# Moving small matmul groups in a fused FFT and gated feed-forward kernel: opening steps and batch 1's slots

## The chip, the cores and the metric

The kernel runs on one core of a Trainium2 chip. The metric is the device time of one execution in microseconds. Five engines work side by side and synchronise by semaphores: TensorE (PE; its weight loads are PEld), VectorE (DVE), ScalarE (ACT), GpSimd (POOL) and SyncE (SP), which issues transfers. A ratio in this document is the mean time of one kernel's fast runs over that of the other's in the same rounds, so it isn't quite the ratio of the medians quoted.

## The reference, cut to what matters

```python
X = np.fft.fft(np.fft.fft(x, axis=1), axis=2).real          # x: 8 x 3008 x 256
x = X.reshape(8 * 3008, 256)
gate = np.maximum(x @ w_gate, 0.0)                           # 256 x 1536
return (gate * (x @ w_val)) @ w_out                          # 1536 x 256
```

## The kernel before

The FFT over the sequence is done in two stages of matmuls (stage one over 94 rows, a shuffle, stage two over 32). The FFT over the 256 columns never happens by itself: it is multiplied into the weights, which is the "W fold". Real input makes half of the rows mirror images of the other half, so one gate tile G and one value tile V serve both: first the direct product is taken, then one more matmul with the mirrored weights `wm` is added to the same tile and the mirrored product is taken. In names, `cs` is 0 or 1 and picks one of two halves of a transform (for the weights, wc or ws). An *evacuation* is the copy of a finished matmul result out of its accumulator buffer. TensorE *stands* when it waits with nothing to do.

A *step* (or slot) is one of 8 x 3 x 12 tiles of 512 columns (batch, block, 128 hidden features). The twelve opening steps (batch 0, block 0) have no output matmuls yet, and the W folds for the features 512 to 1535 are done beside them. Everything else that must happen in between is hung on a slot number (`nyquist`, not shown, is a group of twelve one-column matmuls; `load_x` issues half of a batch's input, a plain part in the queue it is given and a gather of the mirrored part in GpSimd's):

```python
def fold_w(n, i, cs, ps=None):                 # W fold: two f32 matmuls, 64 weight columns each
    ps = ps or spare("psw")                    # one of two spare buffers, in turn
    ...
    nc.scalar.copy((wc, ws)[cs][i][:, sl_], ps[:])
    if cs and (n or i):
        scale_w(n, i, ps)                      # VectorE: wm, from the same buffer

def upright(blk, cs, evac):  ...               # 4 matmuls of 128 columns, then a copy to t4
def rotate(b, a0=0, a1=NKA, evac=...):  ...    # the "turn": one tiny matmul, then a copy
def stage2(b, blk, cs, evac):                  # 4 matmuls of 128 columns, then a copy to pq
    ...
    if cs == 1 and (b or blk):
        row = view(Nd, ...)                    # one 1 KB row goes to DRAM ...
        nc.sync.dma_start(out=row, in_=pq[0:1, 1, :])
        nc.sync.dma_start(out=nbt[b, blk][:], in_=view(row, 0, [[0, 128], [1, 512]]))  # ... and comes back on 128 partitions

for t in range(NF + 1):                        # the opening steps; NF = 12
    if t:      mirror_gate(t - 1)
    if t < NF: gate(t)
    if t:
        value(t - 1, 2)                        # adds the mirrored weights to V of step t-1
        mirror_h(t - 1, 1, nc.vector, pair(t - 1, "V"))
    if t < NF:
        value(t, 0); value(t, 1)
        direct_h(t, 1)                         # VectorE; must read V before value(t, 2) adds to it
        between(t)                             # what is hung on slot t
```

`nb` (the row on 128 partitions) is read by the product E of later steps: `E = nb * af + V`. GpSimd folds the next batch's input (`fold`, 23 pieces a batch) while it also makes one mirrored product per two steps; `FIRST` is how many pieces of batch 1 come before the steps, and `pace` deals out the others.

## Time and profile before

| | before |
|---|---|
| median of the first 4 runs | 625.49 us (625.27 to 626.45) |
| span of the profiled run | 623.2 us |
| first W fold inside the steps | 22.25 us from the start |
| from there to the mirrored V matmul of step 11 | 27.04 us |
| from there to the last matmul | 567.98 us |

The last three rows cut the span at matmuls: the start-up, the opening steps, all else. (Some 6 us from the last matmul's start to the end of the span are left out.) The lines of the profile itself are in the prediction below. In these lines `x4` is a count, the bracket at the end is the engine's idle time just before the line and what ended it, and `xcount` entries are merged neighbours.

### The profile page before, as it was taken

The page shows a single profiled execution, that of the slowest core. Times are in us where ns is not written, and L with a number is a line of the kernel's source. Part 1 is how long each engine was busy: PE and PEld are TensorE (multiplying, and loading weights), DVE is VectorE, ACT ScalarE, POOL GpSimd, SP SyncE. Part 2 cuts the span into 40 slices and gives each one's busy share as a digit, 9 for nine tenths or more (in the row PEclk, how much of TensorE's full clock was granted, in tenths as well). Part 3 has the DMA queues.
Part 4 walks back from the last instruction along what each step waited for, and adds up shares of the span by engine and source line. Part 5 has one row for each costly group of instructions (what it writes and reads, how often), then busy time and mean ns, then how long its engine had stood idle before and what let it go on. Part 6 is the DMA issues. An engine that isn't in the chain of part 4 may idle for free.

```text
span 623.2 us, 11964 instructions
## 1 busy us (share of the span) xinstructions
PE 614.0 (99%) x4284; PEld 409.6 (66%) x4284; DVE 538.2 (86%) x654; ACT 444.6 (71%) x855; POOL 519.9 (83%) x447
## 2 busy tenths in 40 slices
PE   8999999999999999999999999999999999999996
PEld 5336666766666666666667666666666666666665
DVE  8677997899889898888988998898988889899991
ACT  8667777777777767767677767767677776766661
POOL 8987998998989898998989989898988865565665
PEclk9999999999999999999999999999999999999998
DMA  7885274525553183613825255531832134212114
GB/s 169 240 161 118 61 191 113 137 66 160 118 139 84 34 235 83 151 36 89 212 75 126 64 158 123 135 90 34 226 89 49 34 85 117 60 34 67 34 35 100
DMA packets 42038, 67.44 MB, mean 108 GB/s; under 512 B 5877, under 2 KB 31774, under 8 KB 39962
## 3 DMA queue, kind: packets, MB, share of 16 engines
q1 hardware_dynamic: 37162, 50.61, 32.3%
q0 software_dynamic: 4656, 15.88, 10.7%
q8 instruction: 33, 0.54, 0.4%
q14 instruction: 27, 0.22, 0.1%
q10 hardware_dynamic: 160, 0.20, 0.1%
HBM read 38.85 MB, written 30.17 MB: 111 GB/s over the span
## 4 chain that ended last, share of the span: by engine, by line
PE 96%; DVE 2%; ACT 1%; issue 0%; POOL 0%; POOLq 0%; DVEq 0%
PE po L683 40%; PE V L634 20%; PE G L619 10%; PE G L620 10%; PE G L626 10%; PE psw L333 2%; PE ps L162 2%; PE ps L271 2%; DVE h L647 0%; PE pst L240 0%; PE ps L216 0%; ACT t L230 0%; ACT back L197 0%; PE ps L166 0%; DVE wm L327 0%
## 5 line engine op out<-in xcount | busy, mean ns | idle before, releaser
L654 POOL TENSOR_TENSOR h<-gm,E 128x992 bf16<-128x992 f32 (+1 forms) x138 | 320.1, 2319 | 81.8 <-DVE E L661 50.4
L683 PE MATMUL po<-wo,h 128*128 128x256 bf16 (+2 forms) x2304 | 328.5, 272 | 0.0
L683 PEld LDWEIGHTS <-h 128*128 128x128 bf16 (+2 forms) x2304 | 231.4, 103 | 105.9
L628 ACT ACTIVATE gm<-G 128x496 f32<-128x496 f32 (+1 forms) x288 | 170.6, 592 | 94.6 <-PE G L626 87.8
L647 DVE TENSOR_TENSOR h<-gs,V 128x1024 bf16<-128x1024 f32 (+3 forms) x150 | 173.8, 1159 | 58.7 <-PE V L634 39.7
L641 DVE SCALAR_TENSOR_TENSOR E<-nb,af,V 128x496 f32<-128x496 bf16 (+1 forms) x276 | 190.2, 731 | 2.2 <-PE G L620 2.2
L621 ACT ACTIVATE gs<-G 128x497 f32<-128x497 f32 (+2 forms) x288 | 169.6, 589 | 24.7 <-PE G L620 24.7
L661 DVE SCALAR_TENSOR_TENSOR E<-E,V 128x992 f32<-128x992 f32 (+1 forms) x138 | 164.5, 1192 | 0.0
L619 PE MATMUL G<-pq,wc 128*128 128x497 bf16 (+2 forms) x288 | 107.9, 375 | 0.0
L620 PE MATMUL G<-pq,ws 128*128 128x497 bf16 (+2 forms) x288 | 107.9, 375 | 0.0
L626 PE MATMUL G<-pq,wm 128*128 128x496 bf16 (+1 forms) x288 | 107.9, 375 | 0.0
L634 PE MATMUL V<-pq,ws 128*128 128x497 bf16 (+2 forms) x288 | 85.4, 375 | 0.9 <-DVE E L641 0.9
L634 PE MATMUL V<-pq,wc 128*128 128x497 bf16 (+2 forms) x288 | 85.4, 375 | 0.0
L620 PEld LDWEIGHTS <-ws 128*128 128x128 bf16 x288 | 28.2, 98 | 32.7
L696 ACT COPY os<-po 128x512 f32<-128x512 f32 x63 | 37.0, 587 | 14.6 <-PE po L683 12.6
L634 PEld LDWEIGHTS <-wc 128*128 128x128 bf16 x288 | 28.2, 98 | 20.0 <-issue 1.6
L114 POOL TENSOR_TENSOR eo<-xla 94x256 bf16<-94x256 f32 x56 | 40.4, 733 | 0.7
L619 PEld LDWEIGHTS <-wc 128*128 128x128 bf16 x288 | 28.2, 98 | 18.1 <-DVE pq L278 0.8
L114 POOL TENSOR_TENSOR eo<-xlb 94x256 bf16<-94x256 f32 (+1 forms) x42 | 34.5, 822 | 0.9
L111 POOL TENSOR_TENSOR xla<-xla,xha 94x510 f32<-94x510 f32 x28 | 32.9, 1175 | 2.2
L177 ACT CAST t<-ps 96x512 bf16<-96x512 f32 x56 | 32.7, 584 | 2.4 <-PE ps L162 0.2
L626 PEld LDWEIGHTS <-wm 128*128 128x128 bf16 x288 | 28.1, 98 | 4.1 <-issue 1.6
(142 smaller groups left out, 370.8 us busy)
## 6 DMA issues: line engine op xcount, KB each, us to landing
out_dram<-os SPq DMA_DIRECT2D x124, 128.0 KB
Td<-t SPq DMA_DIRECT2D x7, 768.0 KB
t<-Td SPq DMA_DIRECT2D x7, 768.0 KB
out_dram<-os SPq DMA_DIRECT2D x82, 64.0 KB
xla<-in_x_dram SPq DMA_DIRECT2D x7, 720.0 KB
xlb<-in_x_dram SPq DMA_DIRECT2D x6, 640.0 KB
nb<-Nd SPq DMA_DIRECT2D x23, 128.0 KB
out_dram<-os SPq DMA_DIRECT2D x40, 48.0 KB
```

Of the source, the lines that this page charges most:

```text
L114: yield eng.tensor_tensor(e1[:, :, k:k + H], x1[:, :, 0:H], free(x1, D, [DX, n], [-1, H]), op=op)
L619: nc.tensor.matmul(G[:, ds], lhsT=wc[0][:, fs], rhs=pq[:, 0, ds], start=True, stop=False)
L620: nc.tensor.matmul(G[:, ds], lhsT=ws[0][:, fs], rhs=pq[:, 1, ds], start=False, stop=True)
L621: nc.scalar.activation(pair(t, "gs")[:, t % 2, ds], G[:, ds], ACTF.Relu)
L626: nc.tensor.matmul(G[:, cols], lhsT=wm[0][:, f * 128:(f + 1) * 128], rhs=pqt[b, blk][:, 1, cols], start=False, stop=True, skip_group_check ...
L628: nc.scalar.activation(pair(t, "gm")[:, t % 2, cols], G[:, cols], ACTF.Relu)
L634: nc.tensor.matmul(pair(t, "V")[:, t % 2, cs], lhsT=w[:, f * 128:(f + 1) * 128], rhs=pqt[b, blk][:, min(k, 1), cs], start=(k == 0), stop=( ...
L641: nc.vector.scalar_tensor_tensor(pair(t, "E")[:, t % 2, cols], nbt[b, blk][:, cols], af[:, f:f + 1], pair(t, "V")[:, t % 2, cols], op0=ALU ...
L647: nc.vector.tensor_tensor(pair(t, "h")[:, k, 0, 0:ds.stop - ds.start], pair(t, "gs")[:, k, ds], pair(t, "V")[:, k, ds], op=ALU.mult)
L654: eng.tensor_tensor(free(pair(t, "h")[:], 1024 * (t % 2) + 512 + w - 1, [1024, n], [-1, w]), pair(t, "gm")[:, k, cols], val[:, k, cols], o ...
L661: nc.vector.scalar_tensor_tensor(E[:, :, cols], E[:, :, cols], 2.0, V[:, :, cols], op0=ALU.mult, op1=ALU.subtract)
L683: nc.tensor.matmul(po[0:m, i, :], lhsT=pair(t - f + ff, "h")[:, ff % 2, sg, g * 128:g * 128 + m], rhs=wo[:, ff, :], start=(ff == 0), stop= ...
```

## The change

Its intent: turns and second-stage matmuls of batch 0 stand beside the W folds, two evacuations leave VectorE, batch 1's half with the row comes first, its input is loaded ahead of the first fold piece, and its slots move up.

```diff
-FIRST = 15
+FIRST = 17
...
+        load_x(1, 1, pl)
         first = fold(1, pl)
         next(first)
-        load_x(1, 1, pl)
...
     for n in (1, 2):
-        for k, t in enumerate(((0, 1, 2, 3), (4, 5, 6, 7))[n - 1]):
-            at(t, fold_w, n, k // 2, k % 2)
-    for t, blk, cs, e in ((2, 1, 1, "dve"), (4, 1, 0, "dve"), (6, 2, 1, "dve"), (8, 2, 0, "dve")):
-        at(t, upright, blk, cs, e)
-    at(3, rotate, 0, 4, 8)
-    at(7, rotate, 0, 8, NKA)
-    for t, blk, cs, e in ((5, 1, 1, "act"), (9, 2, 1, "act"), (10, 1, 0, "dve"), (11, 2, 0, "act")):
-        at(t, stage2, 0, blk, cs, e)
+        t = 4 * n
+        at(t - 4, fold_w, n, 0, 0)
+        at(t - 3, fold_w, n, 0, 1)
+        at(t - 3 if n == 1 else t - 4, upright, n, 1, "act" if n == 1 else "dve")
+        at(t - 2, rotate, 0, 4 * n, 4 * n + 4)
+        at(t - 2, fold_w, n, 1, 0)
+        at(t - 2, upright, n, 0, "dve")
+        at(t - 1, fold_w, n, 1, 1)
+        at(t - 1, stage2, 0, n, 1, "act")
+        at(t + 1 if n == 1 else t, stage2, 0, n, 0, "act")
     at(8, nyquist)
-    plan = {0: (12, 13, 14, 16, 19, 22, 23, 24), 1: (4, 5, 7, 10, 14, 18, 20, 21)}
+    plan = {0: (12, 13, 14, 15, 17, 20, 21, 22), 1: (4, 5, 7, 10, 14, 18, 20, 21)}
...
-        sh, tr, t2 = (22, 28, (29, 30, 32, 34, 35, 37)) if b else (25, 30, (31, 32, 33, 34, 35, 37))
+        sh, tr, t2 = (22, 28, (29, 30, 32, 34, 35, 37)) if b else (23, 29, (30, 31, 32, 34, 35, 37))
...
-            at(t0 + k, stage2, b + 1, i // 2, i % 2, "act")
+            at(t0 + k, stage2, b + 1, i // 2, 1 - i % 2, "act")
-            for half, k in enumerate((5, 24) if b else (14, 31)):
+            for half, k in enumerate((5, 24) if b else (14, 26)):
...
-        paced["due"] += 0 if t < 12 else 0.8 if t < 23 else 0.75 if t < 54 else 23 / 36
+        paced["due"] += 0 if t < 12 else 0.75 if t < 22 else 0.68 if t < 54 else 23 / 36
```

## The prediction

> **What bounds the kernel now.** I read part 1 of the page first, then the waits, then TensorE's timeline from start to start.
>
> ```profile
> PE 614.0 (99%) x4284; PEld 409.6 (66%) x4284; DVE 538.2 (86%) x654; ACT 444.6 (71%) x855; POOL 519.9 (83%) x447
> ```
>
> TensorE has no neighbour: in a span of 623.2 us only 9.2 us are not covered by its matmuls. That number is not yet a ceiling, because a matmul's box is longer than the place it takes: one of 496 columns is 0.37 us long but its successor starts 0.21 us later. So I took every start-to-start distance and subtracted the columns at 2.4 GHz. From 60 us on the remainder is 0.33 to 0.43 us per 20 us, which is streaming at full speed, except for one 20 us stretch with 1.40 us, where one distance is 1.02 us too long. Before that the remainder is 2.8 us (20 to 40 us) and 2.6 us (40 to 60 us). Only these two places can give anything; the change touches both. First place, TensorE's timeline of the twelve opening steps (batch 0, columns: start, length, engine, line, operation):
>
> ```profile
> 24.62 1.08 PE L333 MATMUL psw<-wst,cd 128*64 128x512 f32 x4
> 25.63 0.38 PE L626 MATMUL G<-pq,wm 128*128 128x496 bf16 x1
> ...
> 26.27 0.37 PE L634 MATMUL V<-pq,wm 128*128 128x496 bf16 x1
> ...
> 26.99 1.08 PE L333 MATMUL psw<-wst,cd 128*64 128x512 f32 x4
> ...
> 32.23 1.08 PE L333 MATMUL psw<-wst,cd 128*64 128x512 f32 x4 [0.17 <-DVE wm L327]
> ...
> 45.73 0.37 PE L634 MATMUL V<-pq,wm 128*128 128x496 bf16 x1
> ...
> 47.51 0.37 PE L634 MATMUL V<-pq,wm 128*128 128x496 bf16 x1
> ...
> 48.13 0.39 PE L271 MATMUL ps<-m,t 128*128 128x128 bf16 x4
> ...
> 49.29 0.37 PE L634 MATMUL V<-pq,wm 128*128 128x496 bf16 x1 [0.53 <-DVE h L647]
> ```
>
> A step with a W fold lasts 26.99 - 24.62 = 2.37 us when nothing else stands in it: the fold 1.01, six matmuls of 0.21, and some 0.1 of unhidden weight load. TensorE is the limit there. A step without a fold (9 to 11) lasts 49.29 - 47.51 = 1.78 us, as did the one before (47.51 - 45.73), although its matmuls need only 1.25 us plus 0.25 for a second-stage group. What sets 1.78 is in VectorE's timeline:
>
> ```profile
> 46.20 0.67 DVE L654 TENSOR_TENSOR h<-gm,V 128x496 bf16<-128x496 f32 x1 [0.53 <-PE V L634]
> 46.79 0.67 DVE L647 TENSOR_TENSOR h<-gs,V 128x496 bf16<-128x496 f32 x1
> 47.37 0.68 DVE L278 CAST pq<-ps 128x512 bf16<-128x512 f32 x1
> 47.98 0.67 DVE L654 TENSOR_TENSOR h<-gm,V 128x496 bf16<-128x496 f32 x1
> ```
>
> The mirrored matmul into V starts at 45.73; VectorE's mirrored product follows 0.47 later; the direct product of the next tile comes 0.59 after it; the next mirrored matmul waits for that one and starts 0.72 later: 0.47 + 0.59 + 0.72 = 1.78. This is a loop between two engines. The evacuation in the third line stands inside its slack and costs nothing: the last loop has no evacuation on VectorE and has the same length.
>
> Second place, the first step of batch 1. SyncE's queue, then VectorE, then TensorE:
>
> ```profile
> 89.30 0.97 SPq L93 DMA_DIRECT2D xlb<-in_x_dram  x2
> 92.76 0.24 SPq L282 DMA_DIRECT2D Nd<-pq  x1
> 98.68 0.35 SPq L283 DMA_DIRECT2D nb<-Nd  x1
> ```
>
> ```profile
> 98.68 1.20 DVE L647 TENSOR_TENSOR h<-gs,V 128x994 bf16<-128x994 f32 x1 [0.37 <-PE V L634]
> 101.65 1.37 DVE L641 SCALAR_TENSOR_TENSOR E<-nb,af,V 128x496 f32<-128x496 bf16 x2 [1.77 <-PE G L620]
> ```
>
> ```profile
> 103.07 0.58 PE L634 MATMUL V<-pq,ws 128*128 128x496 bf16 x2 [0.85 <-DVE E L641]
> ```
>
> The row of second-stage results (cs=1 half) goes to DRAM and comes back as the broadcast nb. It is issued behind 752 KB of x; its write takes 98.68 - 92.76 = 5.9 us until nb can be issued, and nb arrives about 101.6. The wait of 1.77 is put down to a matmul that had long been done (101.18), so it is the DMA. TensorE loses 1.02 us by the start-to-start count (0.85 in the view). Nothing after it loses any.
>
> **What the Trainium skill says.** "Perfetto Trace Analysis", Identifying the Most-Contended Engine: matmul busy share is not a good measure, since matmuls are pipelined; the trace agrees (0.37 against 0.21), hence the counting of starts. "TensorE: Matmul & The Clock Gate", Back-to-back issue gap: N/2.4 + 2.5 ns, 209 ns for 496 columns; the trace has 0.21. "PSUM — Partial Sum Buffer", PSUM bank collisions raise a hardware error: no two engines in one bank and quadrant at once. So ScalarE's copy of a fold and VectorE's scaled copy of it run one after the other: copy 25.75 to 26.34, scale 26.36 to 27.11, and the buffer is free 2.5 us after the fold began. "DMA: Bandwidth & Descriptors", Issuing engines are not separate DMA queues: all transfers share 16 engines and interleave; a 1 KB row needing 5.9 us behind x agrees.
>
> **The change part by part.** No instruction is added or removed; two evacuations move from VectorE to ScalarE.
>
> *Opening steps.* Steps 1 to 8 held four upright groups, two turns, the nyquist group and one second-stage group; steps 9, 10, 11 held one second-stage group each. Now all four second-stage groups are in steps 3, 5, 7, 8. So three groups (0.24, 0.25, 0.25 with the one-column matmuls and a trifle of issue: 0.74 us) leave steps where the 1.78 loop hid them, and enter steps where TensorE is the limit. Against that, waits go: 0.24 before the fold at 32.23 and 0.25 before the upright group at 42.61 (each for the scaled copy of the fold two buffers earlier), 0.05 at 37.46; in sum 0.54. New ones come, because the two spare buffers still alternate and a fold's buffer is free only 2.55 us (for a bf16 group) to 2.62 us (for a fold) after the fold began. Placing the new order by hand from 23.26: the turn of step 2 comes 0.05 too early, the fold of step 6, whose predecessor in the same buffer began 2.4 us before, waits 0.22, the others under 0.03. Sum to step 9: + 0.74 - 0.54 + 0.27, some + 0.5; following it step by step with rounding gives step 9 at 43.9 instead of 43.3. Then three loops of 1.78 in either kernel. So batch 0's opening becomes **0.55 us longer**, not shorter.
>
> *Row and x of batch 1.* The cs=1 half of block 0 moves from slot 32 to slot 30: 91.72 to about 87.7, plus 0.55 = 88.2. Its copy ends near 89.4, the row goes out near 89.9 behind the stores of 86.95. Even with 5.9 us for the write and 2.6 for the broadcast nb lands at 98.4; VectorE can use it from 99.9 + 0.55. The x half that stood in front of the row is issued at slot 26, some 9 us earlier. So the 1.02 us go whole: **-1.0 us**.
>
> *Slots moved up, x before the fold, FIRST and pace.* GpSimd loses 1.48 us waiting for x at 30.9; the issue of the other half (2.8 us) now fills this, which pays for the two extra fold pieces (about 2.1 us). The last pieces of batch 1's fold should end near 66.7 (71.3 now), and stage one asks for them near 68 to 72.5. The shuffle starts at about 74 instead of 77.84; its two transfers took 4.8 and 4.3 us, so it is back by 83 and the turn at slot 29 (about 85.9) finds it; now 87.0 meets 87.63. At the slower pace later folds end up to 0.8 piece (about 2 us) later; the least slack I find for the sixth product of batch 2 is 5.3 us (132.2 against 137.5). Worth on the path: **0**.
>
> Sum: + 0.55 - 1.02 = -0.47 us of 625.5, 625.0 us.
>
> **Rivals.** (1) *The opening gains.* If evacuations on VectorE lengthened steps 9 to 11, removing them would give those steps' waits back (0.27 + 0.28 + 0.70 by the start-to-start count): 623.2 to 623.8 in all. For it: the view blames VectorE's product. Against it: two loops, one with and one without an evacuation, are both 1.78. (2) *ScalarE becomes the bound of steps 1, 3, 5, 7*, with two copies beside two activations: four operations at a spacing of 0.48 are 1.9 us, below 2.6, but they delay the mirrored product by 0.5 us of a slack of about 0.8. If it binds, + 0.2 to + 0.5 per step: 626 to 627. (3) *A new wait in batch 1*: fold pieces or the shuffled tile late for the earlier slots, since x, stores and shuffle now overlap: up to + 1, cancelling the second gain: 626.0.
>
> **Range and chances.** The two sums are both fractions of a microsecond; the three runs of before spread over 1.2 us. I place the range a little lopsided to the fast side for rival 1: 624.0 to 626.1. A change of 2% would be 12.5 us, more than all the idle time TensorE has; slower by that needs a mechanism that I don't see. Faster 0.005, same 0.985, slower 0.01.
>
> **What would show it.** After: steps without fold still 1.78 apart from one mirrored V matmul to the next; the first V matmul of slot 12 at about 49.8 (49.29 now); a wait of some 0.2 before the fold of step 6; no gap of TensorE between 100 and 105, with E in VectorE's timeline following its predecessor directly and the row's write issued near 90. It is wrong if steps 9 to 11 fall below 1.7, if the opening ends before 49.3, if TensorE still waits for E at batch 1, or if a new wait appears between 60 and 100.

## The result

The changed kernel took 625.16 us (median of 4 runs, 624.65 to 625.70) against 625.49 us; ratio 0.9992, interval 0.9975 to 1.0009. Repeated later in 5 rounds: 625.02 against 625.54 us, ratio 0.9992, interval 0.9978 to 1.0005. By its times it is the same (the interval reaches from 1.6 us faster to 0.6 us slower); by the traces the whole stretch from the first W fold in the steps to the last matmul went from 595.02 to 594.65 us, which is 0.37 us less, and again 594.66 in the second trace of the changed kernel. The profiled run of the first result happens to have the later start-up (23.05 us), so its span, 623.9 us, is longer than that of before.

Part 1 of the changed kernel's page:

```profile
PE 612.0 (98%) x4252; PEld 409.3 (66%) x4284; DVE 536.7 (86%) x652; ACT 445.5 (71%) x857; POOL 520.0 (83%) x447
```

TensorE's count is 4252 and not 4284: 32 matmul records are missing from this trace, while the weight loads are all there. That makes holes of 0.22 us, exactly one matmul long, at regular places in a start-to-start count, and 2 us less of busy time. Neither is real. VectorE has two instructions fewer and ScalarE two more: the two evacuations.

TensorE's timeline of the opening steps, after (columns as in the prediction):

```profile
25.42 1.08 PE L333 MATMUL psw<-wst,cd 128*64 128x512 f32 x4
26.44 0.40 PE L240 MATMUL pst<-perm,t 128*128 128x128 bf16 x4
...
38.78 1.08 PE L333 MATMUL psw<-wst,cd 128*64 128x512 f32 x4 [0.20 <-DVE wm L327]
...
47.18 0.37 PE L634 MATMUL V<-pq,wm 128*128 128x496 bf16 x1 [0.24 <-DVE h L647]
...
48.96 0.37 PE L634 MATMUL V<-pq,wm 128*128 128x496 bf16 x1 [0.36 <-DVE h L647]
...
50.74 0.37 PE L634 MATMUL V<-pq,wm 128*128 128x496 bf16 x1 [0.79 <-DVE h L647]
```

In the second line an upright group follows the fold, where in the kernel before the next G matmul followed (25.63): TensorE fills such a step, so the group adds its own time. The third line has the new wait of step 6. The last three are 1.78 us apart as before, and the idle time before them has grown (0.24 and 0.36 where the view of before showed none, 0.79 where it showed 0.53): the groups that had stood there were free. VectorE, after:

```profile
47.66 0.67 DVE L654 TENSOR_TENSOR h<-gm,V 128x496 bf16<-128x496 f32 x1 [0.53 <-ACT gs L621]
48.24 0.66 DVE L647 TENSOR_TENSOR h<-gs,V 128x496 bf16<-128x496 f32 x1
49.44 0.67 DVE L654 TENSOR_TENSOR h<-gm,V 128x496 bf16<-128x496 f32 x1 [0.53 <-PE V L634]
```

The evacuation that stood between the second and third line is gone, and the third line still starts 1.78 after the first. SyncE's queue and VectorE at batch 1, after:

```profile
83.02 1.70 SPq L93 DMA_DIRECT2D xlb<-in_x_dram  x2
...
90.73 0.23 SPq L282 DMA_DIRECT2D Nd<-pq  x1
93.46 0.34 SPq L283 DMA_DIRECT2D nb<-Nd  x1
```

```profile
100.14 1.20 DVE L647 TENSOR_TENSOR h<-gs,V 128x994 bf16<-128x994 f32 x1 [0.41 <-PE V L634]
101.24 1.37 DVE L641 SCALAR_TENSOR_TENSOR E<-nb,af,V 128x496 f32<-128x496 bf16 x2
```

The row leaves at 90.73 (92.76 before, although this run started 0.8 us later), its write takes 93.46 - 90.73 = 2.7 us and not 5.9, and E follows its predecessor without a wait. TensorE has no standing there.

### The profile page after: what moved, and what is told of

It reads as the page before. It is cut to its first block, busy times and chain, and to the rows that moved or that the text cites. A ratio compares the mean times of both kernels' runs of the same rounds, so it can differ in the third digit from the quotient of the medians.

```text
span 623.9 us, 11929 instructions
## 1 busy us (share of the span) xinstructions
PE 612.0 (98%) x4252; PEld 409.3 (66%) x4284; DVE 536.7 (86%) x652; ACT 445.5 (71%) x857; POOL 520.0 (83%) x447
## 4 chain that ended last, share of the span: by engine, by line
PE 96%; DMA 1%; POOL 1%; issue 1%; DVE 1%; ACT 0%; POOLq 0%; DVEq 0%
PE po L683 40%; PE V L634 19%; PE G L619 10%; PE G L626 10%; PE G L620 10%; PE psw L333 2%; PE ps L162 2%; PE ps L271 2%; DMA lo<-in_x_dram 1%; POOL hi L132 0%; DVE h L647 0%; PE pst L240 0%; PE ps L216 0%; PE ps L166 0%; POOL lo L129 0%
## 5 line engine op out<-in xcount | busy, mean ns | idle before, releaser
L619 PE MATMUL G<-pq,wc 128*128 128x496 bf16 (+2 forms) x287 | 107.6, 375 | 1.2
L634 PE MATMUL V<-pq,ws 128*128 128x496 bf16 (+2 forms) x280 | 83.7, 374 | 0.0
L634 PE MATMUL V<-pq,wc 128*128 128x496 bf16 (+2 forms) x266 | 80.7, 374 | 0.0
```

The costliest lines, as they stand in the source:

```text
L619: nc.tensor.matmul(G[:, ds], lhsT=wc[0][:, fs], rhs=pq[:, 0, ds], start=True, stop=False)
L634: nc.tensor.matmul(pair(t, "V")[:, t % 2, cs], lhsT=w[:, f * 128:(f + 1) * 128], rhs=pqt[b, blk][:, min(k, 1), cs], start=(k == 0), stop=( ...
```

## The experiments

All twelve traces, cut at the same three matmuls (us). Single runs: their times are not compared closely, only their traces.

| kernel | start-up | opening | rest | opening + rest |
|---|---|---|---|---|
| before | 22.25 | 27.04 | 567.98 | 595.02 |
| after | 23.05 | 27.69 | 566.96 | 594.65 |
| opening_only | 22.38 | 27.69 | 568.39 | 596.09 |
| batch1_only | 22.53 | 27.04 | 566.96 | 594.00 |
| evac_only | 22.20 | 27.04 | 567.72 | 594.76 |
| loop_filled | 22.58 | 26.19 | 567.21 | 593.40 |
| x_slot_only | 22.97 | 27.03 | 572.23 | 599.26 |
| cs_first_only | 23.24 | 27.18 | 567.63 | 594.81 |
| slots_only | 22.49 | 27.69 | 566.96 | 594.66 |
| x_behind | 22.67 | 27.69 | 566.96 | 594.65 |
| after_again | 22.37 | 27.70 | 566.96 | 594.66 |
| loop_filled_again | 22.71 | 26.19 | 567.21 | 593.40 |

The theory is that of the prediction: the opening loses, batch 1's row gains, the other slots are worth nothing on the path. Its rivals are the three of the prediction.

### opening_only: the opening's order alone

Edit: on the kernel before, only the two blocks of `at(...)` lines of the opening steps from the diff above.

> Before, with the change's order of the twelve opening steps alone. My theory: three second-stage groups leave the loop of 1.78 us and enter steps that TensorE fills, so from the first W fold in the steps to the last mirrored V matmul of step 11 it takes 27.6 to 27.7 us (27.04 before), TensorE still stands about 1.0 us for E at batch 1, and the whole is 0.6 us slower than before (626.1). Rival 1 (the opening gains because evacuations leave VectorE): under 26.5 us there and 624.3 in all.

Measured: 625.95 us against 625.35 (4 and 9 runs), ratio 1.0008, interval 0.9993 to 1.0023. By the times that is the same within noise. By the trace the opening takes 27.69 us, 0.65 more than before, and TensorE stands 1.14 us for E at batch 1 (and 0.27 us at the turn of slot 30, see cs_first_only below). Rival 1 would have had under 26.5 us, and falls.

### batch1_only: all but the opening's order

Edit: on the changed kernel, the opening's `at(...)` lines of before.

> The changed kernel with the old order of the opening steps. My theory: the opening is back at 27.0 us, no standing of TensorE near 100 to 105 us, so 1.0 us faster than before and 0.6 faster than the changed kernel: ratio 0.9983 to before. Rival 1: as slow as before less 1.0, but slower than the changed kernel. Rival 3 (a new wait in batch 1): any gap of TensorE over 0.3 us between 50 and 105 us other than missing matmul records.

Measured: 624.33 us against 625.35 (5 and 9 runs), ratio 0.9986, interval 0.9972 to 1.0000. The opening is back at 27.04 us exactly, the rest at 566.96 exactly. The two parts of the change add up: + 0.65 in the opening, - 1.02 in the rest. Between 50 and 105 us no gap of TensorE over 0.3 us is left, so rival 3 does not occur here.

### evac_only: two evacuations moved and nothing else

```diff
-    for t, blk, cs, e in (..., (8, 2, 0, "dve")):      # upright
+    for t, blk, cs, e in (..., (8, 2, 0, "act")):
-    ..., (10, 1, 0, "dve"), ...                        # stage2
+    ..., (10, 1, 0, "act"), ...
```

> Before, with only the two evacuations (second upright group of block 2, cs=0 half of block 1) given to ScalarE in their old slots. My theory: the mirrored V matmuls of steps 8 to 11 stay 1.78 us apart and the opening stays at 27.0 us. Rival 1: the spacing of steps 9 and 10 falls below 1.6 us, the opening to under 26.5 us.

Only one of these two is an evacuation that the change moves: the cs=0 half of block 1. The change's other one is the first upright group of block 1, in step 1; here the one of step 8 is moved instead, just before the steps that rival 1 speaks of.

Measured (one run, 624.71 us): the spacings of the last three mirrored V matmuls are 1.79, 1.78 and 1.78 us, and the opening is 27.04 us. Taking work off VectorE in these steps changes nothing. What rival 1 would call VectorE's load is a loop between VectorE and TensorE. In this run the standing at batch 1 was 0.48 us and not 1.02: the arrival of nb varies from run to run (1.14 in opening_only). Another 0.27 us stands at the turn of slot 30, as in opening_only.

### loop_filled: the groups where the loop leaves room

```diff
-    (the change's opening block)
+        for k in range(4):
+            at(4 * n - 4 + k, fold_w, n, k // 2, k % 2)
+    at(1, upright, 1, 1, "act")
+    at(3, upright, 1, 0, "act")
+    at(8, upright, 2, 1, "act")
+    at(8, rotate, 0, 4, 8)
+    at(9, stage2, 0, 1, 1, "act")
+    at(9, upright, 2, 0, "dve")
+    at(10, stage2, 0, 1, 0, "act")
+    at(10, rotate, 0, 8, NKA)
+    at(11, nyquist)
+    at(11, stage2, 0, 2, 1, "act")
+    at(18, stage2, 0, 2, 0, "act")
```

(The last one uses the buffer that the output matmuls are not using, as later batches do.)

> The changed kernel, with the opening groups put where the 1.78 loop leaves TensorE 0.5 us a step: nothing but the two upright groups of block 1 beside W folds; turns, block 2's upright groups, second stage and nyquist in steps 8 to 11, the cs=0 half of block 2 in slot 18. My theory: the opening takes 25.8 us (27.04 before, 27.69 after), slot 18 costs 0.25, batch 1 keeps its gain: 2.0 us faster than before, ratio 0.9968, 623.5 us. If the loop isn't the limit but TensorE's sum of work is, the opening stays near 27.0 to 27.7 us. If the added groups lengthen the loop itself, its spacing rises over 2.0 us in steps 8 to 11 and the opening to over 26.7 us.

Measured: 623.73 us against 625.35 (5 and 9 runs), ratio 0.9978, interval 0.9965 to 0.9992: faster, clear of noise, though far below 2%. The opening takes 26.19 us, 0.85 less than before and 1.50 less than after; the rest has 567.21, 0.25 more than 566.96, as expected of slot 18. The opening was expected at 25.8. Of the 0.39 us missing, 0.27 is in step 8; the rest was not traced (the kernel's timeline, all engines, cut):

```profile
41.46 0.75 DVE L327 TENSOR_SCALAR wm<-psw,s 128x512 bf16<-128x512 f32 x1 [0.60 <-ACT ws L336]
...
42.13 0.66 DVE L654 TENSOR_TENSOR h<-gm,V 128x496 bf16<-128x496 f32 x1
...
42.70 0.66 DVE L647 TENSOR_TENSOR h<-gs,V 128x496 bf16<-128x496 f32 x1
...
43.42 0.37 PE L634 MATMUL V<-pq,wm 128*128 128x496 bf16 x1 [0.19 <-DVE h L647]
```

The mirrored V matmul of step 7 starts at 41.37 and its product could start 0.47 later, at 41.84. VectorE is still at the scaled copy of the last fold and starts it at 42.13, so this turn of the loop is 43.42 - 41.37 = 2.05 us and not 1.78. In this loop an operation on VectorE is free only where it fits between the direct product and the next mirrored one; this one didn't. The three turns after it are 1.78 again, although step 9 now holds eight matmuls of 128 columns (five before, one of them of a single column).

### x_slot_only, cs_first_only, slots_only: which part moved the row

Three kernels with one look each. The first two are the kernel before with a single line of the diff; the third is the changed kernel with two lines put back.

```diff
 x_slot_only    -  (14, 31)              +  (14, 26)
 cs_first_only  -  i // 2, i % 2         +  i // 2, 1 - i % 2
 slots_only     -  i // 2, 1 - i % 2     +  i // 2, i % 2
                -  (14, 26)              +  (14, 31)
```

> Before, with the second x half of batch 2 issued at slot 26 instead of 31, nothing else. Theory (the row's write was held up by x): the row is still issued near 92.8 us, but its write takes about 2.7 us as in the changed kernel and not 5.9, nb is issued near 95.5, and TensorE's gap of 1.0 us near 102 is gone. But here the shuffle's second transfer, which took from 82.7 to 87.0 us, now shares the engines with 1.5 MB of x: I expect it to land 1 to 3 us later and TensorE to stand as long before the turn of slot 30 (87.6 us). If x had no part in it, the write still takes over 5 us.

Measured (630.02 us against 625.39, one run each): the row's write takes 1.1 us and TensorE does not stand for E. But it stands at the turn of batch 1, and so the row was issued at 98.74 and not near 92.8 us, when no x was in transit any more (DMA share 0.00 from 96 to 98 us). What x at slot 26 alone does to a row at 92.8 this run therefore doesn't show. TensorE's timeline there, then the windows (columns: window, its length, busy time of PE, PEld, DVE, ACT, POOL with instruction counts, granted clock, DMA share, GB/s):

```profile
91.93 0.19 PE L259 MATMUL psr<-t,rot 128*128 128x12 bf16 x1 [3.42 <-DMA t<-Td]
```

```profile
88.00:92.00 4.00, 0.58 (x7) 0.28 (x6) 2.26 (x3) 0.69 (x2) 3.92 (x4) 1.00 1.16 249
92.00:96.00 4.00, 4.00 (x21) 2.45 (x22) 0.00 (x0) 1.87 (x4) 3.26 (x3) 0.57 0.75 205
```

The shuffled tile was issued at 84.00; the 8 KB pieces of GpSimd's gather of x land from 84 to 87 us, the shuffle's 512-byte pieces mostly from 87 to 90. The standing by start-to-start count is 3.6 us, somewhat above the 1 to 3 expected, and there is a second cost that I had not foreseen: in the 4 us after it the granted clock is 0.57, worth 4 x 0.43 = 1.7 us. Sum 5.3, and 572.23 - 566.96 = 5.27. The Trainium skill ("TensorE: Matmul & The Clock Gate", HAM oscillation — how this bites in real kernels) gives the rule "no PE-idle gaps >~3.4µs"; this gap (3.42 us in the view, 3.6 by the start-to-start count) agrees, and the standing of 1.0 us in the kernel before did not lower the clock (1.00 from 102 to 104 us). No gap between these two was measured.

> Before, with the cs=1 half first from batch 1 on, nothing else. Theory: the row is issued at 90.3 instead of 92.76 us but still right behind x in the same queue, so nb's issue moves from 98.7 only to about 97, and a gap of TensorE of 0 to 0.7 us near 102 remains (1.0 before). If the order alone is what mattered: nb is issued under 94.5 us and there is no gap.

Measured (625.91 us against 625.39, one run each): I missed. The standing for E is gone, not reduced, with nb issued at 95.58 (94.6 with the later start-up of 1.0 us taken off). SyncE's queue in this kernel:

```profile
92.00 0.23 SPq L282 DMA_DIRECT2D Nd<-pq  x1
95.58 0.34 SPq L283 DMA_DIRECT2D nb<-Nd  x1
96.09 0.89 SPq L93 DMA_DIRECT2D xlb<-in_x_dram  x2
```

In slot 31 the stage-two group is hung before the x load, so with the row in slot 31 SyncE issues the row, waits for it, issues nb, and only then gets to x. The order in which SyncE issues, not the two microseconds, decided it: x moved behind the row. The write still took 3.6 us; the 8 KB pieces of GpSimd's gather, the other part of that load, landed meanwhile, from 92 to 95 us. The time did not improve, because TensorE stood elsewhere in this run, at the turn in slot 30, 0.67 us by the start-to-start count:

```profile
89.42 0.19 PE L259 MATMUL psr<-t,rot 128*128 128x12 bf16 x1 [0.50 <-DMA t<-Td]
```

Up to there this kernel is the kernel before, instruction for instruction. The kernel before, then, has a turn that is reached just when the shuffled tile lands (87.0 against 87.63 us in its own trace), and in some runs stands for it: 0.67 us here, 0.27 in evac_only and in opening_only, nothing in its own trace.

> The changed kernel with the cs=0 half first again and the second x half back at slot 31; its earlier slots of stage one, shuffle, turn and second stage stay. Theory: the row is issued near 91.5 us, behind x issued near 90; its write takes 4 to 6 us, and TensorE stands 0 to 0.7 us near 102. If the earlier slots are what matters: write under 3 us, no gap.

Measured (625.02 us against 625.39, one run each): missed too. SyncE's queue:

```profile
91.31 0.23 SPq L282 DMA_DIRECT2D Nd<-pq  x1
92.41 0.34 SPq L283 DMA_DIRECT2D nb<-Nd  x1
92.92 0.88 SPq L93 DMA_DIRECT2D xlb<-in_x_dram  x2
```

The row's write takes 1.1 us, x is issued behind nb, and nothing stands: rest 566.96. The reason is the one of cs_first_only: here too the row's slot is 31, the slot of x. So the swap of halves and the earlier slots each remove the standing for E by themselves, by putting the row ahead of x. For the earlier x that isn't shown, since the standing at the turn delayed the row. Of the three, only the earlier slots also make room for the turn; moving x alone takes that room away.

### x_behind: x of batch 1 not ahead of the fold

```diff
-        load_x(1, 1, pl)
         first = fold(1, pl)
         next(first)
+        load_x(1, 1, pl)
```

> The changed kernel with the second x half of batch 1 behind the first fold piece, as before. Theory: GpSimd idles about 1.5 us before its first fold piece again and ends batch 1's fold up to 1.5 us later (67.6 in the changed kernel), which the slots of stage one still bear: no new gap of TensorE over 0.3 us, opening 27.7 us, same time as the changed kernel within 0.3 us from the first W fold to the last matmul. Rival: a gap of 0.3 to 1.5 us between 60 and 75 us.

Measured (625.12 us against 625.39, one run each): opening 27.69, rest 566.96, no gap. GpSimd's first piece of batch 1, in this kernel and then in the changed one:

```profile
32.39 0.21 POOL L109 TENSOR_TENSOR xla<-xla,xha 94x4 f32<-94x4 f32 x1 [1.40 <-DMA xha<-in_x_dram,ix]
```

```profile
31.37 1.42 POOL L93 DMA_DIRECT2D xlb<-in_x_dram  x2
33.10 1.00 POOL L96 DMA_INDIRECT xhb<-in_x_dram,ix  x1 [0.30 <-issue]
34.12 0.22 POOL L109 TENSOR_TENSOR xla<-xla,xha 94x4 f32<-94x4 f32 x1
```

The idle 1.40 us of the first is filled by the issue of x in the second. At the end of batch 1's fold the difference is small (44.5 us after the start-up in either kernel: 67.17 - 22.67 and 67.56 - 23.05), because GpSimd waits for E in between. On the path this part is worth nothing, as predicted.

### after_again and loop_filled_again

> The changed kernel unaltered, to set it beside loop_filled on one chip. From the first fold to the last matmul as in its first trace (27.7 us opening, no gap at batch 1); ratio to before 0.9993 (0.4 us faster), with the start-up before the first fold scattering by up to 1 us between runs as in all traces so far (22.2 to 23.2 us).

> loop_filled unaltered, in the same rounds: 1.3 us faster than the changed kernel by the traces (1.5 us in the opening less 0.25 for the group in slot 18), so ratio to before 0.9972. If the start-up scatter hides it, the intervals overlap and only the traces decide.

Measured on one chip in the same rounds: the changed kernel 625.02 us, ratio 0.9992 (0.9978 to 1.0005); loop_filled 623.99 us, ratio 0.9976 (0.9962 to 0.9990); before 625.54 us (9 runs). loop_filled is faster than the kernel before, clear of noise in both series, by about a quarter of a per cent. Against the changed kernel the intervals overlap, and the traces decide: 593.40 and 594.66, 1.26 us, the same in both pairs of traces to 0.01 us.

## Why the prediction was right or wrong

**The total.** 625.0 was predicted and 625.16 measured (0.47 us less expected, 0.37 us less by the traces). The total alone proves little, as the measured interval takes in no change at all. But the two terms can be checked one by one in the traces.

**Batch 1's row: right.** - 1.02 us was predicted, 567.98 - 566.96 = 1.02 measured. With the later start-up of 0.8 us taken off, the row's issue at 90.73 is 89.9 as predicted, the turn at 86.74 is 85.9 as predicted, and the shuffle at 74.47 is 73.7 (74 predicted). (The x load came 7.1 us earlier by the same reckoning, 9 predicted.) What the prediction did not see is that its cause is overdetermined: it argued from the x load 9 us earlier and the row 3.5 us earlier, and the runs show that the earlier slots alone, or the swap of halves alone, would do, because SyncE then issues the row before x. Whether the earlier x alone would do is open. It also gave the turn of the kernel before a tight fit (87.0 against 87.63) without saying that a fit like that fails in some runs.

**The opening: mechanism right, size a little off.** + 0.55 us was predicted, + 0.65 measured, in opening_only, after and after_again alike. The loop of 1.78 us is confirmed by evac_only, by the grown idle times of the changed kernel, and by loop_filled. The mis-sized term is "Sum to step 9: + 0.74 - 0.54 + 0.27", which is 0.47: to the mirrored V matmul of step 8 it measured 45.40 - 24.70 = 20.70 after against 43.94 - 23.90 = 20.04 before, so + 0.66. Up to the G matmul at 43.30, where the prediction ends its sum, it was nearly right (44.62 less the later start-up of 0.80 is 43.82: + 0.52, with the wait in step 6 at 0.25 us by the start-to-start count and not 0.22). The other 0.14 lies behind that point: the mirrored V matmul of step 8 waits 0.14 us for VectorE, which the prediction left out. ScalarE's and VectorE's timelines, after:

```profile
43.12 0.75 DVE L327 TENSOR_SCALAR wm<-psw,s 128x512 bf16<-128x512 f32 x1 [0.73 <-ACT ws L336]
43.46 0.60 ACT L628 ACTIVATE gm<-G 128x496 f32<-128x496 f32 x1
44.09 0.67 DVE L654 TENSOR_TENSOR h<-gm,V 128x496 bf16<-128x496 f32 x1 [0.22 <-PE V L634]
```

In step 7 ScalarE has two copies ahead of the mirrored activation, which ends at 44.06. The mirrored product on VectorE follows at 44.09, 0.82 after its V matmul at 43.27 (0.73 in the same step of the kernel before, 0.47 in the loop); VectorE itself was at a scaled copy until 43.87. So this is rival 2, ScalarE's two copies, in one step of four and below the 0.2 to 0.5 us that I gave it. That is read from the trace; no run took the copies away. The prediction had said they "delay the mirrored product by 0.5 us of a slack of about 0.8"; in step 7 the slack was smaller, because the next step has no fold.

**The zero for slots, x and pace: right.** x_behind and batch1_only show no gap between 50 and 105 us, and the rest is the same 566.96 in every kernel with the earlier slots and no group in slot 18. This holds for the parts together: FIRST and pace were never varied alone.

**Rivals.** Rival 1 fell in opening_only and evac_only. Rival 3 did not occur in the changed kernel, but x_slot_only shows that it is real one line away. What remains argued and not shown is the scatter of the start-up; its waits for the first x differ from trace to trace, but no run here varied them on purpose.

## What to carry to other kernels

Before moving work out of a stretch with idle time, find out which limit sets the length of each stretch: moving matmuls from steps held by a two-engine loop into steps that TensorE fills made this kernel's opening longer, and moving them the other way made it 0.85 us shorter than before. Look at the order in which an engine issues its transfers: whether a 1 KB row or 752 KB of input went first decided here whether TensorE stood for a microsecond, even within one slot. Cut traces at instructions that all variants share; here that turned a difference lost in 1 us of start-up scatter into one reproducible to 0.01 us.

## What the Trainium skill lacked or had wrong

- "TensorE: Matmul & The Clock Gate", Back-to-back issue gap: the sustained figure of about 131 ns per matmul at N=512 and 81 ns at N=128 for streams of weight load and matmul isn't met here. Each of the streamed 496-column matmuls with its own weights takes 0.21 us start to start, more than 131 ns, and four of 128 columns take 0.24 us together, 0.06 each and less than 81 ns; the isolated formula N/2.4 + 2.5 ns comes near both (209 and 56 ns).
- The same section has no figure for f32. A pair of f32 matmuls of 512 columns with 64 weight columns each took 1.01 us to the start of the next bf16 matmul (24.62 to 25.63 in the kernel before).
- "DMA: Bandwidth & Descriptors", Anatomy of one DMA: its fit, a fixed 2.0 us and a part that grows with the bytes, is for transfers issued by GpSimd; the section has none for SyncE's, and no term for other traffic. A 1 KB row issued by SyncE took 1.1 us (slots_only, x_slot_only), 3.6 us (cs_first_only, a gather landing meanwhile) and 5.9 us (before, behind x) between its issue and the issue that waits for it.
